# Strassen's identity for the gate and value products of the last two blocks, with GpSimd making sums

## The chip, the cores and the metric

The kernel runs on one core of one Trainium2 chip. The metric is the device time of one execution in microseconds. The core has five engines with queues of their own: TensorE (PE; its weight loads are shown as PEld), VectorE (DVE), ScalarE (ACT), GpSimd (POOL) and SyncE (SP, which issues most DMAs here). Each engine works through its own queue in order and waits for the others through semaphores.

## The reference

Linear attention with cosine weights, followed by a gated feed-forward layer:

```
phi(x) = [relu(x) * cos, relu(x) * sin]           # cos, sin of the position; 64 -> 128 features
kv  = phi(k)^T v ;  z = sum over positions of phi(k)
x   = (phi(q) kv) / (phi(q) z + 1e-6)             # 8 batches x 8 heads x 576 positions x 64
g   = x @ w_gate ;  val = x @ w_val               # x: 4608 x 512, weights 512 x 1536
out = (gelu(g) * val) @ w_out                     # w_out: 1536 x 512
```

Inputs and output are float32; the kernel multiplies in bf16 and accumulates in float32.

## The kernel before

The 4608 tokens of x are cut into nine blocks of 512 (NB = 9). For each block, `gv_unit` makes 128 of the 1536 columns of gate and value: four matmuls of 512 columns with w_gate into one PSUM bank and four with w_val into the next (line 401), then gelu on ACT (line 409), then the multiply on DVE that writes `hT` (line 410). Twelve such units (jt = 0 to 11) make a block. The units alternate between banks 0 and 1 and banks 2 and 3, so a unit may start once the unit before the last has been read out.

The output product of a block is made while the next block's units run. It already uses Strassen's identity in Winograd's form: per half p of a block, seven products of 128 x 768 by 768 x 256 in place of eight. `product` (line 510) issues six matmuls of 256 columns; ACT copies some of the results (line 530), DVE adds them (line 524). The sums of parts of `hT` that the products need, S1 to S4 for each p, are made by `h_sum` on DVE (line 494), and the sums T1 to T4 of w_out were made once, in block 1. PSUM banks 4 and 5 hold the products.

The order of the work is written out by hand: the program order of the loops is the order in each engine's queue (`manual_schedule`), and the semaphore waits follow from the tiles that are read and written. A tile pool with `bufs=2` gives the same two buffers in turn; a new tile of a name waits until the readers of the tile two before it are done. An engine whose next instruction has all its waits fulfilled may run ahead of the others; nothing else ties it to a place in the loop.

The attention of the batches is spread over the blocks before they are needed: DVE and ACT make phi(q) and phi(k) (lines 163 and 161), DVE casts v (line 180), PE makes kv (line 242) and the numerators (line 283), DVE divides (lines 294 to 296), and DMA transposes on SP's queue turn x into `xT` (line 350). This work ends in block 6 (n = 6); blocks 7 and 8 only have gate, value and output products. SP's queue also stores the outputs (line 421). POOL issues the early loads of weights and inputs, until 45 us, and computes nothing after that.

After the last unit, fourteen products of the last block remain: the tail, written as a list at the end of the program. For that block S1, S2 and S4 are made in two pieces, the larger one ahead of the last unit, the rest (the last two jt) in the tail; their place is the free input buffers of q, k and v (`place`).

The lines of the change are `place` and `h_sum` (lines 473 to 494), the main loop (from line 743) and the tail (from line 826).

Of the kernel before, what the change touches and what calls it, by code (L numbers as in the profile page):

```python
# [9 lines left out]
FP32 = mybir.dt.float32  # L10
BF16 = mybir.dt.bfloat16
AF = mybir.ActivationFunctionType
ALU = mybir.AluOpType
# [3 lines left out]
def kernel(  # L17
# [13 lines left out]
    nc = tc.nc  # L31

    B, H, S, D = q.shape
    F = 2 * D
    C = H * D
    J = moe_w_gate.shape[1]
    CT = C // 128
    JT = J // 128
    NP = H // 2
    R = S // 64  # L40
    NB = B * S // 512
    NT = 5
    EPS = 1e-6
    BLK = 512
# [6 lines left out]
    inp = ctx.enter_context(tc.tile_pool(name="inp", bufs=2))  # L51
    attn = ctx.enter_context(tc.tile_pool(name="attn", bufs=1))
# [12 lines left out]
    def bank(i):  # L65
        return ps[:, i]
# [356 lines left out]
    def flush(engs=(nc.sync, nc.sync)):  # L423
        for i, o_sb in stores:
            store(engs, i, o_sb)
        stores.clear()
# [45 lines left out]
    def place(n, p, name, cols, dtype):  # L472

        if n < NB - 1:
            return sums.tile([128, cols], dtype, name=name)
        was = "q" if name[0] == "u" else "kv"[p]
        if was not in rest:
            n_el = 8 * CH if was == "q" else 4 * JH * 128
            rest[was] = [inp.tile([128, n_el], dtype, name=was + "f"), 0]
        t, at = rest[was]  # L480
        rest[was][1] += cols
        return t[:, at:at + cols]

    def h_sum(n, p, name, j0=0, j1=JH):
        a = hs.setdefault((n, p), h_parts(n, p))
        if name not in a:
            a[name] = place(n, p, name, JH * 128, BF16).rearrange("q (j t) -> q j t", j=JH)
        x, y, op = {
            "S1": ("A21", "A22", ALU.add),
            "S2": ("S1", "A11", ALU.subtract),  # L490
            "S3": ("A11", "A21", ALU.subtract),
            "S4": ("A12", "S2", ALU.subtract),
        }[name]
        nc.vector.tensor_tensor(a[name][:, j0:j1], a[x][:, j0:j1], a[y][:, j0:j1], op=op)  # L494

    PROD = {
        1: ("A11", "B11"), 2: ("A12", "B21"), 3: ("S4", "B22"), 4: ("A22", "T4"),
# [5 lines left out]
    def product(n, p, i, u, m, v):  # L503


        a, b = PROD[i]
        key = n, p
        at = {1: u, 6: u, 7: u, 5: m, 3: m, 2: v, 4: v}[i]
        for j in range(JH):
            nc.tensor.matmul(  # L510
                at,
                lhsT=hs.setdefault(key, h_parts(n, p))[a][:, j],
                rhs=ts[b][:, j],
                start=(j == 0 and i in (1, 2, 4, 5)),
                stop=(j == JH - 1),
                skip_group_check=i in (3, 6, 7),
            )
        if key not in got:
            got[key] = [outp.tile([128, C], FP32, name="o_sb") for _ in range(2)]
        lo, hi = got[key]  # L520
        last = n == NB - 1

        def add(o, k, x, op=ALU.add):
            nc.vector.tensor_tensor(o, got[key, k], x, op=op)  # L524

        if i in (1, 6, 7) or last and i == 5:
            if last and i == 7:
                add(hi[:, RIGHT], 5, u)
            got[key, i] = place(n, p, f"u{i}", CH, FP32)
            nc.scalar.copy(got[key, i], at)  # L530
        if i == (2 if last else 1):
            add(lo[:, LEFT], 1, v)
        if i == 7 and not last:
            add(hi[:, RIGHT], 7, m)
        if i == 4:
            add(hi[:, LEFT], 7, v, ALU.subtract)
        if i == 3:
            add(lo[:, RIGHT], 6, m)
        if i in (3, 4):
            flush()  # L540
            stores.append((4 * n + 2 + p, hi) if i == 4 else (4 * n + p, lo))
            if last:
                flush((nc.sync, nc.scalar if p == 1 and i == 4 else nc.sync))


    HALF = BLK // 2
# [193 lines left out]
        (2, 1): ((8,), ()),  # L740
    }
    turn[0] = 1
    for n in range(1, NB):
        b = n + 1

        t_kv, t_nm, t_turn = {1: (7, 9, 12), 2: (6, 7, 11), 3: (2, 5, 9)}.get(n, (1, 2, 8))
        for jt in range(JT):
            if n == 1 and jt >= t_nm:
                nm_unit(2, jt - t_nm, (6, 4, 6)[jt - t_nm])
                turn_x(2, jt - t_nm)  # L750
            heads = (0, 2, 4, 2)[n] if n < 4 else 0
            if n == NB - 1 and jt in (8, 9):
                h_sum(n, jt - 8, "S3")
            if n == NB - 1 and jt == JT - 1:
                for p in range(2):
                    for name in ("S1", "S2", "S4"):
                        h_sum(n, p, name, 0, JH - 2)
            if jt >= heads:
                gv_unit(n, jt)
            else:  # L760
                for i in range(2):
                    half, unit = divmod(2 * jt + i, heads)
                    gv_unit(n, unit, half * HALF, HALF)
                    if n == 1:
                        j = JA + 2 * jt + i
                        prep("q", b, 1, (j,), eng=nc.scalar)
                        prep("q", b, 0, (j,))
                        if jt == i == 0:
                            turn_x_pe(1, 3, 5, act_copy)
            if n > 1:  # L770
                p, u = divmod(jt, 6)
                for i in ((2, 1), (5,), (6,), (7,), (4,), (3,))[u]:
                    product(n - 1, p, i, ps[:, 4, 0:CH], ps[:, 5, 0:CH], ps[:, 4, CH:C])
                for i in map(int, SUMS[n].get(jt, "")):
                    h_sum(n - 1, i // 5, f"S{(i - 1) % 4 + 1}")
            if jt % 3 == 1:
                flush()
            if b < B:
                if n == 1 and jt == 2:
                    prep("q", b, 0, (R - 1,))  # L780
                    prep("q", b, 1, (R - 1,), eng=nc.scalar)
                    turn_q(b)
                    nm_unit(1, NT - 1)
                if n == 1 and jt == 3:
                    turn_x(1, NT - 1)
                nms = [(b, jt - t_nm)] if n > 1 and 0 <= jt - t_nm < NT else []
                if n == 2 and jt < 2:
                    nms.append((n, 3 + jt))

                late = -(-(BLK - 64 * b) // 128)  # L790
                i = jt - t_nm - 1
                if n > 1 and 0 <= i < late:
                    turn_x(b, i)
                if n == 1 and jt == JT - 1:
                    loads(3, ("k", "v"))
                for bt in nms:
                    nm_unit(*bt)
                if jt == t_kv:
                    kv_unit(b)
                if n == 1 and jt in (2, 3, 4):  # L800
                    prep_third("k", b, jt - 2)
                if n == 1 and jt == 5:
                    cast_v(b, 0, 4, dve_copy)
                if (n, jt) in q3:
                    cosines, sines_ = q3[n, jt]
                    prep("q", 3, 1, sines_, eng=nc.scalar)
                    prep("q", 3, 0, cosines)
                for name, c, what in COMING.get(n, {}).get(jt, ()):
                    if name == "v":
                        cast_v(c, what, what + 2, dve_copy)  # L810
                    else:
                        prep(name, c, 0, what)
                        prep(name, c, 1, what, eng=nc.scalar)
                c = {(2, 1): 2}.get((n, jt), b if n > 1 and jt == t_turn else None)
                if c is not None:
                    if c + 1 < B:
                        turn_q(c + 1)
                    if c + 2 < B:
                        loads(c + 2)
                    for i in range(-(-(BLK - 64 * c) // 128), NT):  # L820
                        turn_x(c, i)
            if n == 1 and 4 <= jt < 8:
                wo_sum(f"T{jt - 3}")


    for what in (
        ["S1", "S2", "S4", (0, 1), (1, 1), (0, 2, 0 + 2 * (turn[0] % 2)), (0, 5), (0, 6)]
        + ["T1", "T2", "T4", (1, 2, 1 + 2 * (turn[0] % 2)), (0, 3), (0, 7), (1, 5), (0, 4, 0)]
        + [(1, 6), (1, 3), (1, 7), (1, 4, 1)]
    ):  # L830
        if isinstance(what, str):
            h_sum(NB - 1, "ST".index(what[0]), "S" + what[1], JH - 2, JH)
        else:
            p, i = what[:2]
            to = (what[2:] or (0,))[0]
            product(
                NB - 1, p, i, ps[:, 4 + 2 * p, 0:CH], ps[:, 5 + 2 * p, 0:CH], ps[:, to, 0:CH]
            )


# [28 lines left out]
```

## Time and profile before

| what | value |
|---|---|
| median of 3 runs | 318.86 us (318.25 to 319.17) |
| the profiled execution | 319.06 us, of which the profile's span is 316.9 us |
| PE busy | 306.9 us, 97% |
| DVE busy | 224.7 us, 71% |
| ACT busy | 159.4 us, 50% |
| POOL busy | 26.0 us, 8%, all in the first 50 us |
| granted TensorE clock | 0.996 |
| gate and value matmuls (line 401) | 881 recorded, means of 363 and 364 ns |
| product matmuls (line 510) of 256 columns | mean of 273 ns |
| multiply into hT (line 410) | mean 648 ns |
| product copy on ACT (line 530), sum on DVE (line 524) | means 372 and 418 ns, 256 columns |
| sum of hT parts (line 494), 768 columns | mean 552 ns |

Matmuls are pipelined, so the mean time of one record is longer than the distance to the next. The chain of waits gives the pace: it lists stretches of PE work with their length and the number of matmuls in them. PE's last matmul of a gate-and-value unit ends at 302.4 us; the tail of fourteen products takes 9.18 us after that.

### The profile page before, as it was taken

To read this page: it belongs to the slowest core of one execution; us is meant where nothing else is said; L and a number is where in the kernel's file an instruction comes from. 1 tells how busy PE (TensorE), PEld (TensorE's weight loads), DVE (VectorE), ACT (ScalarE), POOL (GpSimd) and SP (SyncE) were. 2 spreads that over 40 slices of the span, in tenths; PEclk is the share of its full clock that TensorE was granted. 3 is DMA by queue.
4 is the path that set the end of the run, shared out by engine and by line. 5 is a ranking of instruction groups with operands and counts; after the bars stand their busy time and mean duration, and the time that the engine had idled before them with its cause. 6 is when DMAs were issued, how large, how long until landed. Compare 5 with 4: busy or idle time off the path is not lost.

```text
span 316.9 us, 7015 instructions
## 1 busy us (share of the span) xinstructions
PE 306.9 (97%) x2692; PEld 191.8 (61%) x2727; DVE 224.7 (71%) x542; ACT 159.4 (50%) x356; POOL 26.0 (8%) x43
## 2 busy tenths in 40 slices
PE   8899999999999999999999999999999999999994
PEld 2574455655866676666665566556666565656583
DVE  5854695699897996798687859695944554454782
ACT  7864675956474754466328632773232323232321
POOL 6674430000000000000000000000000000000000
PEclk9999999999999999999999999999999999999998
DMA  7999999871798946995993699175342020202025
GB/s 268 245 178 245 312 320 402 259 149 38 241 202 300 304 99 179 370 163 133 319 272 88 152 369 232 34 150 109 76 86 50 17 68 0 66 2 67 2 67 132
DMA packets 68945, 53.61 MB, mean 169 GB/s; under 512 B 45360, under 2 KB 54064, under 8 KB 68912
## 3 DMA queue, kind: packets, MB, share of 16 engines
q1 hardware_dynamic: 59184, 41.23, 49.7%
q0 software_dynamic: 9648, 11.80, 16.1%
q8 instruction: 21, 0.34, 0.4%
q10 hardware_dynamic: 80, 0.13, 0.1%
q14 instruction: 12, 0.10, 0.1%
HBM read 37.75 MB, written 9.44 MB: 149 GB/s over the span
## 4 chain that ended last, share of the span: by engine, by line
PE 86%; DMA 8%; issue 1%; DVE 1%; POOL 1%; SPq 0%; ACT 0%; DVEq 0%; POOLq 0%
PE ps L401 56%; PE ps L510 23%; DMA qf<-in_q_dram 4%; PE ps L283 3%; PE ps L242 2%; DMA vf<-in_v_dram 2%; DMA wv_sb<-in_moe_w_val_dram 2%; PE ps L373 1%; PE ps L431 1%; PE ps L358 0%; DVE x_sb L296 0%; SPq L81 0%; POOL wg_sb L95 0%; DVE o_sb L524 0%; POOL gate L560 0%
## 5 line engine op out<-in xcount | busy, mean ns | idle before, releaser
L410 DVE TENSOR_TENSOR hT<-gel,ps 128x512 bf16<-128x512 f32 (+1 forms) x114 | 73.5, 648 | 55.8 <-PE ps L401 50.3
L401 PE MATMUL ps<-xT,wv_sb 128*128 128x512 bf16 (+1 forms) x450 | 109.4, 364 | 0.3
L401 PE MATMUL ps<-xT,wg_sb 128*128 128x512 bf16 (+1 forms) x431 | 107.4, 363 | 1.5 <-issue 0.3
L409 ACT ACTIVATE gel<-ps 128x512 f32<-128x512 f32 (+1 forms) x114 | 64.4, 566 | 78.6 <-PE ps L401 72.3
L401 PEld LDWEIGHTS <-wv_sb 128*128 128x128 bf16 x456 | 44.6, 98 | 47.1
L401 PEld LDWEIGHTS <-wg_sb 128*128 128x128 bf16 x456 | 41.7, 98 | 28.2 <-issue 0.3
L510 PEld LDWEIGHTS <-S 128*128 128x128 bf16 x336 | 32.9, 98 | 14.9 <-DVE S L494 0.9
L530 ACT COPY u<-ps 128x256 f32<-128x256 f32 x42 | 15.6, 372 | 43.4 <-PE ps L510 43.4
L510 PE MATMUL ps<-T,S 128*128 128x256 bf16 x252 | 34.4, 273 | 0.0
L161 ACT ACTIVATE qp<-qf,sin_t 128x256 bf16<-128x256 f32 x72 | 32.0, 501 | 3.7 <-DMA qf<-in_q_dram 3.7
L524 DVE TENSOR_TENSOR o_sb<-u,ps 128x256 f32<-128x256 f32 x56 | 23.4, 418 | 14.4 <-ACT u L530 14.4
L510 PEld LDWEIGHTS <-hT 128*128 128x128 bf16 x288 | 28.2, 98 | 8.8
L161 ACT ACTIVATE kp<-kf,sin_t 128x256 bf16<-128x256 f32 (+1 forms) x73 | 30.0, 480 | 1.0 <-DMA kf<-in_k_dram 1.0
L296 DVE TENSOR_TENSOR x_sb<-ps,rec 128x512 bf16<-128x512 f32 x38 | 26.3, 692 | 2.0 <-DMA xT<-x_sb 0.5
L163 DVE TENSOR_SCALAR qp<-qf,cos_t 128x256 bf16<-128x256 f32 x71 | 22.0, 357 | 3.3 <-DMA qf<-in_q_dram 3.3
L510 PE MATMUL ps<-wo_sb,hT 128*128 128x256 bf16 x192 | 23.6, 273 | 0.0
L163 DVE TENSOR_SCALAR kp<-kf,cos_t 128x256 bf16<-128x256 f32 x63 | 18.2, 349 | 0.0
L283 PEld LDWEIGHTS <-qT 128*128 128x128 bf16 x304 | 14.6, 98 | 2.8 <-ACT qT L588 0.3
L283 PE MATMUL ps<-kv_sb,qT 128*128 128x65 bf16 x304 | 16.0, 194 | 0.0
L494 DVE TENSOR_TENSOR S<-hT 128x768 bf16<-128x768 bf16 x28 | 15.4, 552 | 0.0
L510 PE MATMUL ps<-T,hT 128*128 128x256 bf16 x96 | 13.1, 273 | 0.2
L180 DVE CAST vx<-vf 128x1152 bf16<-128x1152 f32 (+1 forms) x15 | 11.9, 802 | 1.0 <-DMA vf<-in_v_dram 1.0
(84 smaller groups left out, 204.8 us busy)
## 6 DMA issues: line engine op xcount, KB each, us to landing
out_dram<-o_sb SPq DMA_DIRECT2D x71, 128.0 KB, 2.5
kf<-in_k_dram SPq DMA_DIRECT2D x12, 576.0 KB, 7.2
vf<-in_v_dram SPq DMA_DIRECT2D x12, 576.0 KB, 8.7
qf<-in_q_dram SPq DMA_DIRECT2D x10, 576.0 KB, 5.2
qf<-in_q_dram POOLq DMA_DIRECT2D x4, 576.0 KB, 12.4
kf<-in_k_dram POOLq DMA_DIRECT2D x4, 576.0 KB, 12.5
vf<-in_v_dram POOLq DMA_DIRECT2D x4, 576.0 KB, 12.6
wg_sb<-in_moe_w_gate_dram POOLq DMA_DIRECT2D x6, 256.0 KB, 6.8
```

The costliest lines, as they stand in the source:

```text
L161: nc.scalar.activation(o, i, AF.Relu, scale=tab[:, j:j + 1])
L163: (eng or nc.vector).tensor_scalar(o, i, 0.0, tab[:, j:j + 1], op0=ALU.max, op1=ALU.mult)
L180: copy(vx_tiles[b % 2][:, m0:m1, j0:j1, 0:D], staged["v", b][:, m0:m1, j0 * D:j1 * D].rearrange("p m (j d) -> p m j d", d=D),)
L283: nc.tensor.matmul(bank(b0 + h // 4)[:, (h % 4) * (D + 1):(h % 4 + 1) * (D + 1)], lhsT=q_cols(b, t, h), rhs=kv_sb[b][:, h // 2, h % 2, :], ...
L296: nc.vector.tensor_tensor(x, nm[:, :, :, 0:D], rec[:, :, :, None].to_broadcast([128, 2, 4, D]), op=ALU.mult,)
L401: nc.tensor.matmul(bank(b0 + g)[:, 0:w], lhsT=wt[:, ct, js], rhs=xt[:, ct, c0:c0 + w], start=(ct == 0), stop=(ct == CT - 1),)
L409: nc.scalar.activation(gel[:, 0:w], bank(b0)[:, 0:w], AF.Gelu)
L410: nc.vector.tensor_mul(hT[n][:, jt, c0:c0 + w], gel[:, 0:w], bank(b0 + 1)[:, 0:w])
L494: nc.vector.tensor_tensor(a[name][:, j0:j1], a[x][:, j0:j1], a[y][:, j0:j1], op=op)
L510: nc.tensor.matmul(at, lhsT=hs.setdefault(key, h_parts(n, p))[a][:, j], rhs=ts[b][:, j], start=(j == 0 and i in (1, 2, 4, 5)), stop=(j == ...
L524: nc.vector.tensor_tensor(o, got[key, k], x, op=op)
L530: nc.scalar.copy(got[key, i], at)
```

## The change

Blocks 7 and 8 (`FAST = NB - 2`) no longer use `gv_unit`. Gate and value together are one product of the stacked weights (w_gate over w_val) with x, and Strassen's identity is applied to its halves: the weights' rows are gate or value, the contraction is cut in two (ct 0 and 1, ct 2 and 3), and the block's tokens in two halves of 256. A unit then has seven products of two matmuls of 256 columns each, in place of eight matmuls of 512 columns.

- `w_sum` makes the sums S1 to S4 of the weights on POOL, in twelve pieces of 128 x 1024, written into the loop of block 6 (one in each jt). They lie in the freed input buffers of q, k and v.
- `x_sum` makes T1 to T4 of a block's `xT` on DVE, 128 x 512 each: for block 7 in block 6 at jt 8 to 11, for block 8 in block 7 at jt 2, 4, 6 and 8.
- `fast_unit(t, between)` runs the products of unit t, spread over two units: products 1, 5, 6, 2 and 3 of unit t, and 7 and 4 of unit t - 1. P1 is copied by ACT into the place of P2 in PSUM, and P2 accumulates on it; P6 and P7 and P4 accumulate on P1's bank, P3 on P5's. The out-projection's product of the step before (`o_step`) stands between.
- `h_sum` takes an engine; in blocks 7 and 8 the S sums of `hT` go to POOL. The small rest in the tail stays on DVE.
- The temporaries of the products lie in the buffers of `qT`, `qp` and `kp`; the tail begins inside the last half unit, with (0, 1) ahead of the last P4 and (1, 1) after it.

The core of the diff:

```diff
-    def h_sum(n, p, name, j0=0, j1=JH):
+    def h_sum(n, p, name, j0=0, j1=JH, eng=nc.vector):
...
-        nc.vector.tensor_tensor(a[name][:, j0:j1], a[x][:, j0:j1], a[y][:, j0:j1], op=op)
+        eng.tensor_tensor(a[name][:, j0:j1], a[x][:, j0:j1], a[y][:, j0:j1], op=op)
...
+    def w_sum(name, j0, j1):
+        if not wa:
+            wa["A11"], wa["A12"] = wg_sb[:, 0:CP], wg_sb[:, CP:CT]
+            wa["A21"], wa["A22"] = wv_sb[:, 0:CP], wv_sb[:, CP:CT]
+        if name not in wa:
+            was = {"S1": "qf", "S2": "qf", "S3": "kf", "S4": "vf"}[name]
+            wa[name] = inp.tile([128, CP, J], BF16, name=was)
+        x, y, op = {
+            "S1": ("A21", "A22", ALU.add),
+            "S2": ("S1", "A11", ALU.subtract),
+            "S3": ("A11", "A21", ALU.subtract),
+            "S4": ("A12", "S2", ALU.subtract),
+        }[name]
+        nc.gpsimd.tensor_tensor(
+            wa[name][:, :, j0:j1], wa[x][:, :, j0:j1], wa[y][:, :, j0:j1], op=op
+        )
...
+    GV = {
+        1: ("A11", "B11"), 2: ("A12", "B21"), 3: ("S4", "B22"), 4: ("A22", "T4"),
+        5: ("S1", "T1"), 6: ("S2", "T2"), 7: ("S3", "T3"),
+    }
...
+    def fast_unit(t, between):
+        def at(i, t):
+            if i == 2:
+                return ps[:, 0, 256 * (t % 2):256 * (t % 2) + 256]
+            return bank((3, 1)[t % 2] if i in (3, 5) else (2, 6, 7)[t % 3])[:, 0:256]
+
+        def mm(i, t):
+            n, jt = FAST + t // JT, t % JT
+            a, b = GV[i]
+            for ct in range(CP):
+                nc.tensor.matmul(
+                    at(i, t),
+                    lhsT=wa[a][:, ct, jt * 128:(jt + 1) * 128],
+                    rhs=xb[n][b][:, ct],
+                    start=(ct == 0 and i in (1, 5)),
+                    stop=(ct == CP - 1),
+                    skip_group_check=i not in (1, 5),
+                )
...
+        if new:
+            mm(1, t)
+            nc.scalar.copy(at(2, t), at(1, t))
+            mm(5, t)
+            nc.scalar.copy(tmp(M5, t), at(5, t))
+        if old:
+            mm(7, t - 1)
+            gelu(t - 1, 1, tmp(G2, t - 1))
+            nc.vector.tensor_tensor(tmp(V2, t - 1), tmp(M5, t - 1), at(7, t - 1), op=ALU.add)
+        between()
+        if old:
+            nc.vector.tensor_tensor(
+                h(t - 1, 1), gels[t - 1][:, 256:512], tmp(V2, t - 1), op=ALU.mult
+            )
+        if new:
+            mm(6, t)
+            nc.scalar.copy(tmp(U6, t), at(6, t))
+            mm(2, t)
+            gelu(t, 0, at(2, t))
+            mm(3, t)
+            nc.vector.tensor_tensor(tmp(G2, t), tmp(U6, t), at(3, t), op=ALU.add)
+        if old:
+            mm(4, t - 1)
+            nc.vector.tensor_tensor(
+                h(t - 1, 0), gels[t - 1][:, 0:256], at(4, t - 1), op=ALU.mult
+            )
...
-    for n in range(1, NB):
+    for n in range(1, FAST):
...
+            if n == FAST - 1:
+                w_sum(f"S{jt // 3 + 1}", 512 * (jt % 3), 512 * (jt % 3) + 512)
+                if jt >= 8:
+                    x_sum(FAST, jt - 8)
+
+    def o_step(n, jt):
+        p, u = divmod(jt, 6)
+        for i in ((2, 1), (5,), (6,), (7,), (4,), (3,))[u]:
+            product(n - 1, p, i, ps[:, 4, 0:CH], ps[:, 5, 0:CH], ps[:, 4, CH:C])
+        for i in map(int, SUMS[n].get(jt, "")):
+            h_sum(n - 1, i // 5, f"S{(i - 1) % 4 + 1}", eng=nc.gpsimd)
+        if jt % 3 == 1:
+            flush()
+
+    for t in range(2 * JT):
+        n, jt = FAST + t // JT, t % JT
+        if n == NB - 1 and jt in (9, 10):
+            h_sum(n, jt - 9, "S3", eng=nc.gpsimd)
+        if n == NB - 1 and jt == JT - 1:
+            for p in range(2):
+                for name in ("S1", "S2", "S4"):
+                    h_sum(n, p, name, 0, JH - 2, eng=nc.gpsimd)
+        fast_unit(t, lambda: o_step(FAST + (t - 1) // JT, (t - 1) % JT) if t else None)
+        if n == FAST and jt in (2, 4, 6, 8):
+            x_sum(NB - 1, jt // 2 - 1)
...
+    def ends():
+        o_step(NB - 1, JT - 1)
+        last_product(0, 1)
+
+    fast_unit(2 * JT, ends)
...
-        ["S1", "S2", "S4", (0, 1), (1, 1), (0, 2, 0 + 2 * (turn[0] % 2)), (0, 5), (0, 6)]
-        + ["T1", "T2", "T4", (1, 2, 1 + 2 * (turn[0] % 2)), (0, 3), (0, 7), (1, 5), (0, 4, 0)]
-        + [(1, 6), (1, 3), (1, 7), (1, 4, 1)]
+        [(1, 1), "S1", "S2", "S4", (0, 2, 0), (0, 5), (0, 6), "T1", "T2", "T4"]
+        + [(1, 2, 1), (0, 3), (0, 7), (1, 5), (0, 4, 0), (1, 6), (1, 3), (1, 7), (1, 4, 1)]
```

## The prediction

> **What bounds the kernel now.** I read the page first (engines, slices, chain, groups), then the chain of waits in order of time, the busy time by stretches, and the timelines of the stretches that the change touches. From the page:
>
> ```profile
> span 316.9 us, 7015 instructions
> PE 306.9 (97%) x2692; PEld 191.8 (61%) x2727; DVE 224.7 (71%) x542; ACT 159.4 (50%) x356; POOL 26.0 (8%) x43
> ...
> DVE  5854695699897996798687859695944554454782
> ...
> POOL 6674430000000000000000000000000000000000
> ...
> PE ps L401 56%; PE ps L510 23%; DMA qf<-in_q_dram 4%; PE ps L283 3%; PE ps L242 2%; DMA vf<-in_v_dram 2%; DMA wv_sb<-in_moe_w_val_dram 2%; PE ps L373 1%; PE ps L431 1%; PE ps L358 0%; DVE x_sb L296 0%; SPq L81 0%; POOL wg_sb L95 0%; DVE o_sb L524 0%; POOL gate L560 0%
> ```
>
> PE never rests. POOL is empty after the sixth slice (7.9 us each); DVE is full in the middle and half empty in the last ten slices. In the chain, in order of time, start and length of one gate-and-value unit and of one product:
>
> ```profile
> 278.63 1.73 PE ps L401 x8
> 280.36 0.66 PE ps L510 x6
> ```
>
> Eight matmuls of 512 columns take 1.73 us (0.216 each), six of 256 take 0.66 (0.109 each), each with its own weight load of 98 ns hidden. The last two blocks fill 242 to 302.4 us. The busy time by stretches for one piece of it:
>
> ```profile
> 270.00:280.00 10.00, 9.95 (x62) 5.99 (x62) 4.77 (x9) 2.63 (x5) 0.00 (x0) 1.00 0.23 54
> ```
>
> PE 9.95 of 10 at full clock, DVE 4.8, ACT 2.6, POOL nothing. Less PE work here shortens the kernel, if nothing makes PE wait.
>
> **What the Trainium skill says.** "GPSIMD Engine Reference", section 3.1: a two-input sum on POOL took 4497 ns for 2048 elements a partition, about twice DVE. No such sum is in this trace. "SBUF — State Buffer", section "Who interferes with whom": DVE and GpSimd share a port pair, taken as a lock for a whole instruction, by a DVE instruction in a two-port mode (casts and scalar operations from SBUF) or with two SBUF inputs, against a GpSimd one that reads SBUF. The only place where this trace has both is the start (timeline, start and us):
>
> ```profile
> 4.54 1.86 POOL L163 TENSOR_SCALAR kp<-kf,sin_t 128x128 bf16<-128x128 f32 x1 [2.17 <-DMA kf<-in_k_dram]
> 5.81 0.51 DVE L170 SCALAR_TENSOR_TENSOR kp<-kf,sin_t 128x256 bf16<-128x256 f32 x1
> 6.24 0.41 DVE L170 SCALAR_TENSOR_TENSOR kp<-kf,sin_t 128x256 bf16<-128x256 f32 x1
> ```
>
> POOL needed 1.86 us for 128 columns while DVE ran two-input operations back to back, and the first of two equal DVE operations took 0.10 us more. That agrees with a lock, though weakly: POOL read only 128 columns, so DVE paid little. A two-input sum of 1024 elements would read for all of its two microseconds.
>
> **Part 1, fewer columns.** A unit goes from 8 × 0.216 = 1.73 us to 14 × 0.109 = 1.53: 0.20 saved, times 24 units, **-4.8 us**. Products per block, the tail's 14 products (9.18 us in the chain) and the stores stay.
>
> **Part 2, the new combining work.** Per unit ACT gets five 256-column instructions for one of 512, and half a product copy as before: 5.5 × 0.37 (row L530) = 2.0 us by durations, 1.5 by start to start (two copies in a row take 0.65). DVE gets four for one, and 8 product sums a block: 4.7 × 0.42 (row L524) = 2.0 us, 1.5 by start to start (0.33). The new cycle is 1.53 + 14 × 0.66 / 12 = 2.30 us, so PE still sets it. The tightest wait: P4 of the previous unit overwrites the bank that V2 reads. With PE's unit at 0, P7 ends at 0.66, the product at 1.31, P4 starts at 1.97. V2 follows the previous unit's last multiply on DVE, at about 1.0, and ends at 1.4: 0.55 to spare. U6's copy ends near 1.95 and the next P7 wants it at 2.6. Product sums and the gelu of the other half queue behind V2, and are not nearer. Bounds 0 to 1; I take **+0.3**. The x sums (8 of 512 bf16, 0.42 each) fall where DVE waits 1.0 to 1.7 us a unit; cost nothing. The second block's need xT at about 248 us; the last transpose is issued at 233.6 and the slowest landed in 10.4. No DMA is added and no queue is passed: POOL issues none after 45 us.
>
> **Part 3, the weight sums on POOL.** Twelve of 1024 elements, estimated from the skill's figure at 2.25 us each. They are written in block 6, but POOL's queue is bound only by its waits: S1 takes the slot of q of batch 6, free when ACT's last read ends (173.0), the other nine follow q of batch 7 (203.80 + 1.71 = 205.5). So nine sums run from 205.5 to some 230, where DVE is busiest. From the timelines:
>
> ```profile
> 203.80 1.71 ACT L161 ACTIVATE qp<-qf,sin_t 128x256 bf16<-128x256 f32 x4
> ...
> 206.95 0.87 DVE L163 TENSOR_SCALAR kp<-kf,cos_t 128x256 bf16<-128x256 f32 x3
> ...
> 208.94 0.87 DVE L163 TENSOR_SCALAR kp<-kf,cos_t 128x256 bf16<-128x256 f32 x3
> 209.72 0.76 DVE L180 CAST vx<-vf 128x1152 bf16<-128x1152 f32 x1
> ...
> 214.45 0.55 DVE L494 TENSOR_TENSOR S<-hT 128x768 bf16<-128x768 bf16 x1
> ...
> 215.06 0.72 PEld L510 LDWEIGHTS <-S 128*128 128x128 bf16 x6 [0.15 <-DVE S L494]
> ```
>
> Three groups of prep (three scalar operations, a cast with the second and third) are two-port, then S1 of block 5's h has two SBUF inputs; and PE waits 0.15 us for that S1 already, so each microsecond by which it is late is PE's. By hand, with the lock granted in the order of asking and POOL asking again 0.5 us after it ends: the first group waits from 206.95 to 207.8; the second until 10.9, its cast until 14.0; the third until 16.95, its cast until 20.05; S1 until 23.0 (all + 200) and is done at 223.5 instead of 215.0, 8.5 us late. If each group waits just once, for half a sum: four waits of 1.1 less 1.2 us of idle time in DVE there, 3.3. Without a lock 0. I take **+6**. The three sums at 173 meet nine prep operations and two casts at 174.4 to 180.3; units reuse their banks after about 2.9 us, which covers one wait of 2.25 but not two: 0 to 2.5, **+1**.
>
> **Part 4, h sums moved to POOL.** Eight a block of 768 elements, estimated 1.7 us each for DVE's 0.55. S1 is wanted 3.7 us after h is complete in block 7 and 2.5 in block 8; POOL makes it, by 0.8 there; at 2.6 us it would be 0.1 late. But DVE's multiply of gel and V2 has two SBUF inputs, and everything behind it on DVE (G2, the other multiply, V2 of the next unit, for which P4 waits) moves with it. A wait of up to 1.7 meets 0.55 of cover: the first of a run of sums costs up to 1.2, later ones less, as DVE then follows POOL's rhythm. Two runs, 0 to 3.5 us, **+1.5**. In the tail, POOL's six of 512 elements (1.1 each) run beside DVE's last sums, on which products 5 and 6 wait with about 0.4 us of cover: 0 to 2.5, **+1**.
>
> **Sum:** -4.8 + 0.3 + 6 + 1 + 1.5 + 1 = +5.0. The profiled execution took 319.06 us (span 316.9 and 2.2 around it), so 324.1, and against the median of 318.86, 0.2 lower, **324**.
>
> **Rivals.** *The lock costs little* (chance 0.33): arbitration by burst, a faster sum, or POOL yielding. DVE's 0.10 us at the start speaks for it, POOL's 1.86 against. Then -4.8 + 0.3 + up to 2: 314.4 to 316.5, say 315, faster. It decides at the S1 of 214.45: all lock costs under 3.5 us together make the kernel faster. *DVE nearly holds its own* (0.08): each group waits once; 3.3 + 1 there and elsewhere against 4.5 gained, 318 to 319.8, no change. *DVE becomes the bound in the last blocks without any lock* (0.08): V2 later than its 0.55 of cover by 0.1 to 0.4 in each of 24 units, 2.4 to 10 us, 317 to 324; against it, 1.5 to 2.0 of 2.3 us. *Alternation* (0.09): each two-port operation waits out a sum of its own, eleven times 2.0 us less slack, +12 or more: 331. *The forecast* (0.42): 320 to 330.
>
> **How the numbers follow.** 0.3% of 318.86 (1.0 us) is about what a measurement here can tell from no change. Faster is the first rival and a little of the third, 0.34; same 0.07; slower 0.59. The likeliest case gives 324, its own range 320 to 330. The range must take in the first rival: 314.2 to 330 leaves out alternation and the lowest end, under 2 in 10.
>
> **What would show it.** Right: POOL busy from 173 and from 205.5 on; prep scalar operations and casts there with durations of 1 to 2.5 us in place of 0.35 and 0.76; PE waiting for the S1 of block 6; stretches 242 onward 4 us shorter, yet with DVE waits. Wrong if prep durations hold at 0.35 with POOL busy beside them: then the gain stands. POOL sums far from 2.25 us move every lock term with them; sums of 4.5 would also end after block 7 begins.

## The result, and the profile after

The changed kernel took 334.9 us (median of four runs, 334.41 to 335.17) against 318.56 us for the kernel before beside it (317.65 to 319.17): ratio 1.0514, 95% interval 1.0483 to 1.0544. The profiled span grew from 316.9 to 333.4 us. The forecast was 324.0 us with a range of 314.2 to 330, so the direction was right and the size was not.

From the page of the changed kernel: the engines, three of the lines by fortieths of the span (8.3 us each), and three groups (busy us and mean ns of one behind the bar):

```profile
span 333.4 us, 7614 instructions
PE 308.6 (93%) x2871; PEld 205.8 (62%) x2871; DVE 263.9 (79%) x598; ACT 183.0 (55%) x452; POOL 89.5 (27%) x79
...
PE   8799999999999999999997999818999989999984
...
DVE  5854677898997967986889687898684898888892
...
POOL 5675310000000000000025000994000851194660
...
L568 POOL TENSOR_TENSOR qf<-wv_sb 128x1024 bf16<-128x1024 bf16 x3 | 6.4, 2150 | 128.8 <-ACT qp L161 128.8
...
L163 DVE TENSOR_SCALAR kp<-kf,cos_t 128x256 bf16<-128x256 f32 x63 | 34.2, 600 | 0.0
...
L642 DVE TENSOR_TENSOR hT<-gel,qT 128x256 bf16<-128x256 f32 x24 | 19.2, 799 | 0.8
```

PE's busy time hardly moved (306.9 to 308.6), but PE now rests: the "1" in the 27th slice stands under the second run of POOL work. The prep's scalar operation on DVE (L163) went from a mean of 349 ns to 600. In time order, the chain of waits passes through DVE at that place, and later shows the new unit at its length:

```profile
217.45 4.32 DVE kp L163 x2
221.77 2.59 DVE vx L180
...
280.44 1.53 PE ps L604 x14
```

So the unit did become 0.20 us shorter (1.73 to 1.53), as intended. Where the time went is read from the same instruction in both traces. A ledger of how late the changed kernel is (a matmul is taken to end one step of PE's pace after its start; the last column is rounded from unrounded times):

| the same instruction in both traces | before | after | late by | added in this step |
|---|---|---|---|---|
| DVE multiply for hT, ahead of the first POOL sums | 173.47 | 173.56 | 0.1 | 0.1 |
| DVE multiply for hT, past the three sums at 173 | 206.02 | 209.24 | 3.2 | 3.1 |
| last gate-and-value matmul of block 6 ends, past the nine sums | 242.5 | 258.3 | 15.8 | 12.6 |
| last matmul of all ends, past blocks 7 and 8 and the tail | 312.1 | 328.5 | 16.4 | 0.7 |

Nearly all of the loss, 15.7 of 16.4 us, comes in the two stretches of POOL's weight sums (6.4 us from 173.1 on, 19.6 us from 208.9 on), and none of it on PE's own instructions. The timelines of POOL and of DVE in the second stretch (start, us, engine, line, operation, count; in brackets the idle time before it):

```profile
208.85 6.39 POOL L568 TENSOR_TENSOR qf<-qf,wg_sb 128x1024 bf16<-128x1024 bf16 x3 [29.33 <-ACT qp L161]
215.21 6.41 POOL L568 TENSOR_TENSOR kf<-wg_sb,wv_sb 128x1024 bf16<-128x1024 bf16 x3
221.58 6.88 POOL L568 TENSOR_TENSOR vf<-wg_sb,qf 128x1024 bf16<-128x1024 bf16 x3
```

```profile
210.17 5.22 DVE L163 TENSOR_SCALAR kp<-kf,cos_t 128x256 bf16<-128x256 f32 x3
215.31 0.68 DVE L410 TENSOR_TENSOR hT<-gel,ps 128x512 bf16<-128x512 f32 x1
215.91 0.41 DVE L524 TENSOR_TENSOR o_sb<-u,ps 128x256 f32<-128x256 f32 x1
216.24 5.52 DVE L163 TENSOR_SCALAR kp<-kf,cos_t 128x256 bf16<-128x256 f32 x3
221.69 2.67 DVE L180 CAST vx<-vf 128x1152 bf16<-128x1152 f32 x1
...
225.21 3.66 DVE L163 TENSOR_SCALAR kp<-kf,cos_t 128x256 bf16<-128x256 f32 x3
```

Three scalar operations take 5.22 and 5.52 us in place of 0.87, the cast 2.67 in place of 0.76. Above the times of before that is 4.35 + 4.65 + 1.91 + 2.79 = 13.7 us, of which idle time that DVE had there swallowed 1.1: 12.6. The multiply and the block sum between them, which read PSUM and at most one operand from SBUF, kept their 0.68 and 0.41 us. The prep's operations between 207 and 232 us (count, shortest, median and longest ns) give the rule:

```profile
L163 DVE TENSOR_SCALAR kp<-kf,cos_t x9: 341/2199/2211, 210.2 to 228.5; 128x256 bf16<-128x256 f32 x9
```

2199 ns is one POOL sum of 2150. The first operation of each group took 0.96 to 1.28 us, as it waited out the rest of a running sum; those behind it took 2.20 to 2.21, each a whole sum of its own; the last, at 228.5 past the end of POOL's sums, took its 0.34. Two neighbours among these operations and the POOL sum between them, one record each:

```profile
211.05 2.21 DVE L163 TENSOR_SCALAR kp<-kf,cos_t 128x256 bf16<-128x256 f32 x1
213.07 2.17 POOL L568 TENSOR_TENSOR qf<-qf,wg_sb 128x1024 bf16<-128x1024 bf16 x1
213.18 2.21 DVE L163 TENSOR_SCALAR kp<-kf,cos_t 128x256 bf16<-128x256 f32 x1
```

POOL's next sum starts 0.11 us before DVE's next operation does. DVE has only one operation waiting at a time, and whenever the next one comes, another sum stands ahead of it.

Such waits are the exclusive lock of the Trainium skill, "SBUF — State Buffer", section "Who interferes with whom", and the cases match the section: scalar operations and casts blocked, operations with at most one SBUF input not. It says too that the one that issues first decides who blocks; what happens when POOL has a queue of sums is what this trace adds. The same skill, "Perfetto Trace Analysis", section "GPSIMD Engine Instruction", warns that a POOL duration is unreliable and should be read start to start; here both agree (215.21 - 208.85 is 6.36 for three, 2.12 each). So POOL lost next to nothing by the scalar operations. By the longer cast it did lose; the sum behind it took half a microsecond more:

```profile
223.70 2.63 POOL L568 TENSOR_TENSOR vf<-wg_sb,qf 128x1024 bf16<-128x1024 bf16 x1
```

PE's timeline of the changed kernel shows what the late DVE did to it:

```profile
216.90 0.71 PE L510 MATMUL ps<-wo_sb,hT 128*128 128x256 bf16 x5
225.01 1.68 PE L510 MATMUL ps<-wo_sb,hT 128*128 128x256 bf16 x7 [7.40 <-DVE hT L410]
...
230.99 0.83 PE L510 MATMUL ps<-T,S 128*128 128x256 bf16 x6 [0.89 <-DVE S L494]
```

A product of block 5 stood 7.40 us for an h whose multiply was queued behind the second group and its cast. The matmuls after it ran at about half speed (the granted clock from 220 to 230 us was 0.52), but that cost nothing further, since PE then waited 0.89 us for DVE's S1 all the same.

### The profile page after: what moved, and what is told of

It is laid out like the page before. It is cut to its first block, busy times and chain, and to the rows that moved or that the text cites. A ratio compares the mean times of both kernels' runs of the same rounds, so it can differ in the third digit from the quotient of the medians.

```text
span 333.4 us, 7614 instructions
## 1 busy us (share of the span) xinstructions
PE 308.6 (93%) x2871; PEld 205.8 (62%) x2871; DVE 263.9 (79%) x598; ACT 183.0 (55%) x452; POOL 89.5 (27%) x79
## 4 chain that ended last, share of the span: by engine, by line
PE 74%; DVE 14%; DMA 4%; issue 3%; ACT 2%; POOL 1%; SPq 0%; DVEq 0%; ACTq 0%
PE ps L401 38%; PE ps L510 18%; PE ps L604 8%; DVE kp L163 5%; PE ps L431 3%; PE ps L283 3%; PE ps L242 3%; DMA vf<-in_v_dram 2%; DVE hT L642 2%; DMA wv_sb<-in_moe_w_val_dram 2%; DVE o_sb L524 1%; DVE vx L180 1%; DVE hT L410 1%; ACT qp L161 1%; DVE qT L651 1%
## 5 line engine op out<-in xcount | busy, mean ns | idle before, releaser
L401 PE MATMUL ps<-xT,wv_sb 128*128 128x512 bf16 (+1 forms) x360 | 86.4, 363 | 2.6 <-DVE hT L410 2.6
L401 PE MATMUL ps<-xT,wg_sb 128*128 128x512 bf16 (+1 forms) x360 | 86.5, 363 | 0.5 <-ACT u L530 0.5
L410 DVE TENSOR_TENSOR hT<-gel,ps 128x512 bf16<-128x512 f32 (+1 forms) x90 | 56.8, 635 | 32.0 <-PE ps L401 27.5
L409 ACT ACTIVATE gel<-ps 128x512 f32<-128x512 f32 (+1 forms) x90 | 50.2, 558 | 55.6 <-PE ps L401 50.7
L401 PEld LDWEIGHTS <-wv_sb 128*128 128x128 bf16 x360 | 35.4, 98 | 39.3 <-issue 4.3
L568 POOL TENSOR_TENSOR qf<-wv_sb 128x1024 bf16<-128x1024 bf16 x3 | 6.4, 2150 | 128.8 <-ACT qp L161 128.8
L163 DVE TENSOR_SCALAR kp<-kf,cos_t 128x256 bf16<-128x256 f32 x63 | 34.2, 600 | 0.0
L494 POOL TENSOR_TENSOR S<-hT 128x768 bf16<-128x768 bf16 x8 | 13.6, 1705 | 44.5 <-PE ps L604 43.9
L163 DVE TENSOR_SCALAR qp<-qf,cos_t 128x256 bf16<-128x256 f32 x71 | 21.6, 351 | 2.3 <-ACT kv_sb L251 2.0
L642 DVE TENSOR_TENSOR hT<-gel,qT 128x256 bf16<-128x256 f32 x24 | 19.2, 799 | 0.8
L604 PE MATMUL ps<-qp,qf 128*128 128x256 bf16 x96 | 18.3, 272 | 0.3 <-ACT ps L633 0.3
L604 PE MATMUL ps<-xT,wg_sb 128*128 128x256 bf16 x96 | 18.3, 272 | 0.0
```

The source lines that it names most:

```text
L163: (eng or nc.vector).tensor_scalar(o, i, 0.0, tab[:, j:j + 1], op0=ALU.max, op1=ALU.mult)
L401: nc.tensor.matmul(bank(b0 + g)[:, 0:w], lhsT=wt[:, ct, js], rhs=xt[:, ct, c0:c0 + w], start=(ct == 0), stop=(ct == CT - 1),)
L409: nc.scalar.activation(gel[:, 0:w], bank(b0)[:, 0:w], AF.Gelu)
L410: nc.vector.tensor_mul(hT[n][:, jt, c0:c0 + w], gel[:, 0:w], bank(b0 + 1)[:, 0:w])
L494: eng.tensor_tensor(a[name][:, j0:j1], a[x][:, j0:j1], a[y][:, j0:j1], op=op)
L604: nc.tensor.matmul(at(i, t), lhsT=wa[a][:, ct, jt * 128:(jt + 1) * 128], rhs=xb[n][b][:, ct], start=(ct == 0 and i in (1, 5)), stop=(ct == ...
```

## The experiments

The theory after the result: a run of POOL sums lets in one two-port DVE operation per sum (alternation), and this, not the new units, is the loss. Rivals: the new units make DVE or ACT the bound in the last blocks; the h sums on POOL are the main cost; the loss is the transfers or the place of the sums and not the lock.

**The weight sums alone** (kernel before; the function `w_sum` as in the change, with its tiles in the same slots):

```diff
+            if n == FAST - 1:
+                w_sum(f"S{jt // 3 + 1}", 512 * (jt % 3), 512 * (jt % 3) + 512)
```

> The kernel before with the twelve weight sums on POOL added and nothing else of the change; their results are not used. Theory (port lock, one DVE operation let in per POOL sum): the whole loss of blocks 4 to 6, 3.1 + 12.6 us, comes back: 334 us, prep operations on DVE of 2.2 us at 174 to 180 and 209 to 228. Rival (the new units of blocks 7 and 8 and their waits are to blame, DVE's lag before is only moved): no change from before, 318.6. Rival (POOL and DVE share the port without a lock): 320 to 324.

Measured 334.17 us, ratio 1.0478 (1.0455 to 1.0502). DVE's timeline of this run is the changed kernel's over again:

```profile
209.79 5.22 DVE L163 TENSOR_SCALAR kp<-kf,cos_t 128x256 bf16<-128x256 f32 x3
...
215.86 5.53 DVE L163 TENSOR_SCALAR kp<-kf,cos_t 128x256 bf16<-128x256 f32 x3
```

Twelve POOL instructions, with no other part of the change, make 15.4 us of the 16.3. The rivals that put it into the new units fall.

**The weight sums on DVE** (changed kernel):

```diff
-        nc.gpsimd.tensor_tensor(
+        nc.vector.tensor_tensor(
             wa[name][:, :, j0:j1], wa[x][:, :, j0:j1], wa[y][:, :, j0:j1], op=op
```

> The changed kernel with the twelve weight sums on DVE in block 6 in place of POOL. Theory: the 15.7 us of blocks 4 to 6 go, twelve sums of about 0.7 us find room in block 6: 319 to 320.5, with the 5 us of waits in the last blocks still there. Rival (the new units are to blame): 330 or more.

Measured 320.27 us, ratio 1.0043 (1.0027 to 1.0059). A sum takes DVE 0.68 us, as the first three do (count, shortest, median and longest ns, first and last start):

```profile
L568 DVE TENSOR_TENSOR qf<-wv_sb x3: 683/686/689, 215.0 to 221.5; 128x1024 bf16<-128x1024 bf16 x3
```

Only the last, which met an h sum on POOL, took 2.02. The last gate-and-value matmuls of block 6 start at 241.95, 0.3 us after those of the kernel before (241.64). The loss of 15.8 us there is gone with the same sums, of the same operands, at the same place in the program. It is POOL's part in them that costs. The time changed with the engine, though: DVE comes to these sums from 215.0 us on, when its prep is done. The run with the sums held back moves the time and keeps the engine.

**Half-size sums** (changed kernel, 24 sums of 512 elements):

```diff
-                w_sum(f"S{jt // 3 + 1}", 512 * (jt % 3), 512 * (jt % 3) + 512)
+                for c in (512 * (jt % 3), 512 * (jt % 3) + 256):
+                    w_sum(f"S{jt // 3 + 1}", c, c + 256)
```

> The changed kernel with each weight sum in two halves of 512 elements: 24 sums of 1.1 us. Theory (each two-port operation of DVE waits for one whole POOL sum): eleven waits of 1.1 in place of 2.2 us, so half the lag or less: 324 to 328. Rival (DVE loses what POOL is busy in all, some 26 us, however it is cut): 334 to 335.

Measured 327.78 us (326.14 to 330.39), ratio 1.0286 (1.0222 to 1.035). The line of the prep beside the later sums, the same nine operations as above:

```profile
L163 DVE TENSOR_SCALAR kp<-kf,cos_t x9: 343/1237/1246, 209.5 to 219.6; 128x256 bf16<-128x256 f32 x9
```

The median fell from 2199 to 1237 ns as a POOL sum fell from 2.16 to 1.20 us, and block 6 ended 8.7 us late (250.35 against 241.64) in place of 15.8. POOL had the same elements to sum. What an operation pays follows the length of one POOL instruction, not POOL's total work: this is alternation, one operation to one sum.

**The sums held back** (changed kernel; POOL's queue waits, ahead of its first weight sum, for the last cast of v, at 212.7 us):

```diff
             if n == FAST - 1:
+                if jt == 0:
+                    nc.gpsimd.tensor_copy(gate, vx_tiles[1][:, 3, R - 1, 0:1])
                 w_sum(f"S{jt // 3 + 1}", 512 * (jt % 3), 512 * (jt % 3) + 512)
```

> The changed kernel with POOL held by one small copy until DVE's last cast of v (about 213 us), so that the weight sums run in block 6, where DVE has no two-port operation left, only its h sums with two SBUF inputs. Theory: at most one wait of up to 2.2 us for each of some eight h sums, half of them covered, and S4 perhaps 1 to 2 us late for block 7: 321 to 327. Rival (two-input sums wait no less and everything is only moved): 332 or more.

Measured 323.25 us, ratio 1.0132 (1.0112 to 1.0153). All twelve sums now run from 212.99 to 240.6, past the prep, and block 6 ends 3.0 us late (244.67). The rest of the lock is on DVE's h sums with two SBUF inputs (and on one x sum, 1.63 us). From the timelines of DVE and, in the last line, POOL:

```profile
216.05 1.87 DVE L494 TENSOR_TENSOR S<-S,hT 128x768 bf16<-128x768 bf16 x1
...
217.85 2.47 DVE L494 TENSOR_TENSOR S<-hT 128x768 bf16<-128x768 bf16 x1
...
224.60 0.55 DVE L494 TENSOR_TENSOR S<-hT 128x768 bf16<-128x768 bf16 x1
224.66 2.48 POOL L568 TENSOR_TENSOR qf<-qf,wg_sb 128x1024 bf16<-128x1024 bf16 x1
```

An h sum takes 0.55 us free and up to 2.47 behind a POOL sum. The one at 224.60 started 0.06 us ahead of POOL's next sum and took its 0.55, so the one that asks first goes first. POOL pays here too: eight of its twelve sums took 2.43 to 2.48 us in place of 2.12, as many as there are h sums beside them. One copy of a single element per partition took 11.6 us off the kernel. It is where the sums met DVE's two-port work that cost most.

**Nothing on POOL** (the kernel with the weight sums on DVE, and the h sums of blocks 7 and 8 on DVE as well):

```diff
-            h_sum(n - 1, i // 5, f"S{(i - 1) % 4 + 1}", eng=nc.gpsimd)
+            h_sum(n - 1, i // 5, f"S{(i - 1) % 4 + 1}")
...
-            h_sum(n, jt - 9, "S3", eng=nc.gpsimd)
+            h_sum(n, jt - 9, "S3")
...
-                    h_sum(n, p, name, 0, JH - 2, eng=nc.gpsimd)
+                    h_sum(n, p, name, 0, JH - 2)
```

> The changed kernel with all sums on DVE: the weight sums as in the run before, and the h sums of blocks 7 and 8 too, so that POOL computes nothing. Theory (the waits in the last blocks are the lock's as well, on the multiply of gel and V2): PE's waits there go, most of the 4.8 us saved is seen, less some for a full DVE in block 6: 314 to 316. Rival (the chain of copies, sums and gelus of a unit is itself too long for PE): 318 to 320.5, hardly better than with the h sums on POOL.

Measured 319.36 us (317.39 to 320.78), ratio 1.0015 (0.9998 to 1.0032): a miss by 3.4 us, inside the range of the rival. The trace shows another cause than the rival's. DVE's timeline of this run ahead of the last unit, then PE's:

```profile
298.22 0.42 DVE L494 TENSOR_TENSOR kf<-hT 128x512 bf16<-128x512 bf16 x1
...
300.38 0.42 DVE L494 TENSOR_TENSOR vf<-hT,vf 128x512 bf16<-128x512 bf16 x1
300.73 0.41 DVE L639 TENSOR_TENSOR qT<-qT,ps 128x256 f32<-128x256 f32 x1
```

```profile
301.19 0.38 PE L604 MATMUL ps<-qp,wv_sb 128*128 128x256 bf16 x2 [2.30 <-DVE qT L639]
```

The six sums that POOL had made ahead of the tail now stand in one row in DVE's queue before the next V2 (L639), and PE waits 2.30 us for it. Then the clock fell, in this execution of 320.28 us. PE's stretches after the wait (us in the stretch, busy us and count of PE, PEld, DVE, ACT and POOL; the third number from the right is the granted clock):

```profile
301.00:303.00 2.00, 1.81 (x15) 1.54 (x15) 2.00 (x7) 0.42 (x1) 0.00 (x0) 0.88 0.19 44
303.00:305.00 2.00, 2.00 (x11) 1.35 (x10) 1.42 (x6) 0.37 (x1) 0.00 (x0) 0.50 0.70 162
305.00:307.00 2.00, 2.00 (x16) 1.61 (x14) 0.87 (x3) 0.39 (x2) 0.00 (x0) 0.77 0.25 56
307.00:309.00 2.00, 2.00 (x21) 1.79 (x19) 1.01 (x4) 0.73 (x2) 0.00 (x0) 1.00 0.01 4
```

If the clock is either 1.00 or 0.50, the numbers 0.88, 0.50 and 0.77 come to about 0.5, 2.0 and 0.9 us at half speed: some 3.4 us, from 302.5 on, 1.3 us after the wait ended. The 96 matmuls from 301.19 on took 12.15 us where 96 at 0.109 take 10.5. The wait and the clock together are 2.30 + 1.65 = 3.95 us, about the miss.

The fall seems not to come in every execution of this kernel. Nine of the 22 had a mean granted clock of 0.996 or more and took 317.39 to 319.11 us (median 318.1); thirteen had 0.985 to 0.995 and took 318.9 to 320.78 (median 320.0). That suggests that the wait alone leaves 318.1, 2.1 us above the forecast, and that the clock adds some 1.8 us in part of the executions. Whether this is the order of one queue or a limit of DVE is tried in the run with the late sums spread.

**The sums held back, and the h sums on DVE** (the two edits together):

```diff
+                if jt == 0:
+                    nc.gpsimd.tensor_copy(gate, vx_tiles[1][:, 3, R - 1, 0:1])
...
-                    h_sum(n, p, name, 0, JH - 2, eng=nc.gpsimd)
+                    h_sum(n, p, name, 0, JH - 2)
```

with the other two `eng=nc.gpsimd` left out as in the run before.

> The weight sums on POOL, held until DVE's last cast of v, and the h sums of blocks 7 and 8 on DVE. Theory: block 6 loses 3.0 us as in the run with late sums (323.25), and the last blocks gain what the run without POOL gains: 316 to 318. Rival: as in that run, 322 to 323.

Measured 322.79 us, ratio 1.0128 (1.0096 to 1.0159), a miss by nearly 5 us, inside the range of the rival. Block 6 loses its 3 us as it did with POOL held back alone, and the wait of 2.30 us and the fall of the clock to 0.50 are there again (PE starts again at 304.03, and the clock from 306 to 308 us was 0.50). The expectation left out both, as that of the kernel with nothing on POOL did.

**The h sums on POOL alone** (kernel before, the h sums of blocks 7 and 8 moved):

```diff
-    def h_sum(n, p, name, j0=0, j1=JH):
+    def h_sum(n, p, name, j0=0, j1=JH, eng=nc.vector):
...
-        nc.vector.tensor_tensor(a[name][:, j0:j1], a[x][:, j0:j1], a[y][:, j0:j1], op=op)
+        eng.tensor_tensor(a[name][:, j0:j1], a[x][:, j0:j1], a[y][:, j0:j1], op=op)
...
-                h_sum(n, jt - 8, "S3")
+                h_sum(n, jt - 8, "S3", eng=nc.gpsimd)
```

and the same argument at the two other calls.

> The kernel before with the h sums of blocks 7 and 8 on POOL and nothing else of the change. Theory: DVE's multiply there takes one operand from PSUM and one from SBUF, so no lock is contended, and a sum of 1.7 us is ready in time: 318.5 to 319.5. Rival (any POOL work beside DVE costs): 322 to 325. Rival (the longer sums are late for the products): 320 to 322, with PE waiting on POOL.

Measured 318.4 us, ratio 0.9991 (0.9979 to 1.0002). POOL takes 1.64 us for a sum of 768, and PE isn't delayed: with the old units, DVE in these blocks multiplies out of PSUM with one operand from SBUF, and such a multiply took the same 0.69 us beside a POOL sum as without one. Only in the tail do the two meet; DVE's sums of 256 columns there, from the timeline:

```profile
303.07 1.18 DVE L494 TENSOR_TENSOR kf<-hT 128x256 bf16<-128x256 bf16 x1
304.28 1.20 DVE L494 TENSOR_TENSOR kf<-kf,hT 128x256 bf16<-128x256 bf16 x1
305.51 0.29 DVE L494 TENSOR_TENSOR kf<-hT,kf 128x256 bf16<-128x256 bf16 x1
```

1.2 us in place of 0.29, each behind one POOL sum of 1.15. So h sums on POOL are harmless in themselves; they need an operation with two SBUF inputs on DVE to do harm. Blocks 7 and 8 of the changed kernel have two kinds: gel times V2 (L642) and the x sums (L584).

**Nothing on POOL, with the late sums spread** (the kernel with nothing on POOL; of the six sums in one row one stays, two go behind the last block's first product, and three are made whole in the tail):

```diff
-            for p in range(2):
-                for name in ("S1", "S2", "S4"):
-                    h_sum(n, p, name, 0, JH - 2)
+            h_sum(n, 0, "S1", 0, JH - 2)
...
+        for name in ("S2", "S4"):
+            h_sum(NB - 1, 0, name, 0, JH - 2)
...
-            h_sum(NB - 1, "ST".index(what[0]), "S" + what[1], JH - 2, JH)
+            h_sum(NB - 1, "ST".index(what[0]), "S" + what[1], 0 if what[0] == "T" else JH - 2, JH)
```

> The run without POOL, with the six sums of the last block (0.42 us each, 2.5 us in a row ahead of the last unit's V2) spread: one stays there, two go into the last half unit, the three of p = 1 are made whole in the tail. Theory: in the run without POOL the new units kept pace with PE, and the gain was lost only there, in a PE wait of 2.3 us and some 1.6 us of slower clock after it; without it 315 to 316.5. Rival (the units' own chain of copies and sums eats the gain): 318.5 to 320, no better.

Measured 316.12 us (315.4 to 316.73), ratio 0.9921 (0.9902 to 0.994). This is faster than both kernels. From its page and from the line of the multiply of gel and V2:

```profile
PE 303.1 (97%) x2842; PEld 205.4 (65%) x2871; DVE 250.1 (80%) x631; ACT 183.8 (59%) x452; POOL 28.0 (9%) x43
```

```profile
L642 DVE TENSOR_TENSOR hT<-gel,qT x24: 417/421/429, 247.7 to 301.0; 128x256 bf16<-128x256 f32 x24
```

All 24 of the multiplies take the same 0.42 us. The new units with all their sums fit on DVE, and the rival of the run with nothing on POOL, that a unit's own chain is too long for PE, falls.

**The h sums on POOL, with the late sums spread** (the kernel with the weight sums on DVE, and the edit of the run before; the spread sums are DVE's):

```diff
-                    h_sum(n, p, name, 0, JH - 2, eng=nc.gpsimd)
+            h_sum(n, 0, "S1", 0, JH - 2)
...
+        for name in ("S2", "S4"):
+            h_sum(NB - 1, 0, name, 0, JH - 2)
```

> As the run before, but the h sums of blocks 7 and 8 on POOL, the weight sums and the six late sums on DVE. Theory: POOL's sums of 1.7 us hold up DVE's multiply of gel and V2, which has two SBUF inputs, and PE waits behind it: 2 to 4 us worse than without POOL, 317.5 to 319.5. Rival (the h sums on POOL cost nothing here either, as in the kernel before): 315 to 316.5, the same.

Measured 318.07 us, ratio 0.998 (0.9969 to 0.999). The same line, and two of PE's waits for V2 (L639) with the operation on DVE that came before each, from the timelines:

```profile
L642 DVE TENSOR_TENSOR hT<-gel,qT x24: 415/426/1692, 250.0 to 304.7; 128x256 bf16<-128x256 f32 x24
```

```profile
246.75 1.86 DVE L584 TENSOR_TENSOR qp<-xT,qp 128x512 bf16<-128x512 bf16 x1
249.32 0.38 PE L604 MATMUL ps<-qp,wv_sb 128*128 128x256 bf16 x2 [0.76 <-DVE qT L639]
...
293.02 1.54 DVE L642 TENSOR_TENSOR hT<-gel,qT 128x256 bf16<-128x256 f32 x1
295.62 0.38 PE L604 MATMUL ps<-qp,wv_sb 128*128 128x256 bf16 x2 [0.53 <-DVE qT L639]
```

The theory named half of it. At 293 us it is the multiply, 1.54 us in place of 0.42, that makes the next V2 late for PE's P4. The longest wait, at 249 us, comes from an x sum of 1.86 us in place of 0.42, ahead of which the last weight sum on DVE had already taken 2.03 behind POOL's first h sum. The wait next in length, at 254.39, follows an x sum of 1.20. The h sums on POOL cost about 2.0 us (318.07 - 316.12) in blocks 7 and 8 and the tail, and what they delay are DVE's operations with two SBUF inputs, not the multiply alone.

## Why the prediction was wrong

Its sum of +5.0 us stands against +16.4 at the last matmul. By its parts:

| part of the prediction | its term, bounds | measured |
|---|---|---|
| 1, fewer columns | -4.8 | -4.7: blocks 7 and 8 and the tail are 69.6 us before, and 64.9 of pure matmul time after |
| 2, combining work | +0.3, 0 to 1 | +1.4: PE's gaps in the units with nothing on POOL |
| 3, nine sums at 205 | +6, 0 to 8.5 | +12.6 |
| 3, three sums at 173 | +1, 0 to 2.5 | +3.1 |
| 4, h sums on POOL | +1.5, 0 to 3.5 | +2.3: gaps in the units 3.7 us, less the 1.4; the x sums have a part in it |
| 4, the tail | +1, 0 to 2.5 | +1.7: gaps in the tail |

The lengths of gaps are worked out from PE's timeline: the start of a group less the starts before it at 0.109 us each. The pure matmul time is 24 units of 14 matmuls and 43 products of six at that pace.

**The step that failed is the hand queue of part 3.** The mechanism, the place, the durations of the sums (2.25 us estimated from the Trainium skill, "GPSIMD Engine Reference", section 3.1, and 2.15 measured) and the late S1 of block 5's h were right. (PE stood still earlier than forecast, 7.40 us for the multiply ahead of that S1 in the same queue, and then 0.89 us for S1 itself.) What failed is the line "with the lock granted in the order of asking and POOL asking again 0.5 us after it ends". With those 0.5 us a group of three scalar operations slips through behind one wait, and eleven two-port operations wait only some six times. In the trace POOL has no such pause: its sums start every 2.12 us at a length of 2.15, the next one starts 0.11 us ahead of DVE's next operation, and so DVE gets in one operation per sum. The order of asking was right (the h sum that asked first in the run with the sums held back went first); the pause was not there. Each group then pays twice or more. That is the rival called alternation, with its "eleven times 2.0 us less slack, +12 or more"; 12.6 came, at a chance of 0.09. The half-size sums confirm it: with sums half as long, the delay of an operation halves. The choice of 0.5 us rested on no line of the trace. The bound should have been worked out with 0 as well: by the same hand queue, one operation per sum, S1 comes some 12 us late, and with the other terms at their upper ends the sum is -4.8 + 1 + 12 + 2.5 + 3.5 + 2.5 = +16.7, which draws the range past 334.

The three sums at 173 failed by the same step. They cost 3.1 us, above the 2.5 of "one wait but not two": a single group of prep there took 5.18 us in place of 0.87, 4.3 more, of which the idle time of DVE took 1.2:

```profile
174.50 5.18 DVE L163 TENSOR_SCALAR kp<-kf,cos_t 128x256 bf16<-128x256 f32 x3
```

**Part 1** is right, and the fastest run shows it as a gain. **Part 2** was undersized: 1.4 us where 1 was the upper end. In the run that gives this number DVE makes the h sums too, so it is an upper value for the combining work alone. It consists of 0.44 us at the first unit, for ACT's copy of P1, and of starts of P4 held up by V2 as named, by 0.42, 0.37, 0.09 and 0.09 us; the other units follow each other without a gap. The two longer ones speak against "The x sums [...] cost nothing": each follows an x sum that stands right ahead of V2. DVE's timeline of the fastest kernel ahead of the first of them, an x sum (L584) and V2 (L639), and PE's P4:

```profile
250.62 0.42 DVE L654 TENSOR_TENSOR hT<-gel,ps 128x256 bf16<-128x256 f32 x1
250.95 0.42 DVE L584 TENSOR_TENSOR qp<-xT 128x512 bf16<-128x512 bf16 x1
251.28 0.42 DVE L639 TENSOR_TENSOR qT<-qT,ps 128x256 f32<-128x256 f32 x1
...
251.76 0.38 PE L604 MATMUL ps<-qp,wv_sb 128*128 128x256 bf16 x2 [0.26 <-DVE qT L639]
```

DVE has no pause there: with the h sums of the block before in the same queue, the x sum takes time from V2 and not from a wait. The rival that DVE becomes the bound without a lock thus has a grain of truth, worth about one microsecond of the +16.4. **Part 4** was right about the multiply and left out the x sums, which have two SBUF inputs as well: two of them took 1.75 and 1.20 us in the changed kernel, behind POOL's h sums. Its terms were 0.8 and 0.7 us short.

The rivals that the lock costs little or that DVE nearly holds its own are refuted by the changed kernel's own trace and by the two runs that have the twelve sums as the one difference (+15.4 us alone; -14.6 us when DVE makes them).

What stays open: why a POOL sum loses next to nothing to a scalar operation of 0.35 us, and 0.3 to 0.5 us to an h sum of 0.55 or a cast of 0.76, was seen and not explained. In the fastest kernel two gaps of 0.30 us remain where the last block ends. Both follow the late h sums that DVE still makes there. P4 of the last unit but one starts at 298.35, when V2 has ended at 298.30 behind one of them. A weight load (PEld) waits for the last multiply (L654), which stands behind the other two:

```profile
301.81 0.10 PEld L510 LDWEIGHTS <-hT 128*128 128x128 bf16 x1 [0.41 <-DVE hT L654]
```

## What to carry to other kernels

Work given to an idle engine isn't free if it shares a port with a busy one: when GpSimd has a row of SBUF sums ready, count up to one whole GpSimd instruction for each two-port or two-SBUF-input operation of DVE that meets them, and don't let a queue model give DVE a pause that no trace shows. A queue with nothing ahead of it starts as early as its buffers allow, so ask where it will run and not where it is written; a single-element copy that waits for the right event can hold it back. Before moving work off an engine, try it there in good order: here DVE takes all of the sums, if they don't stand in a row ahead of what PE waits for (six cost 2.30 us, one still 0.30).

## What the runs showed of the hardware that was not expected

- POOL sums without a pause let in DVE's two-port operations one by one. The measured time of such an operation is that of one POOL sum (2199 ns beside 2150), though alone it takes 348 ns. POOL keeps its pace of 2.12 us a sum beside these scalar operations; behind a cast a sum took 2.63, and beside DVE's h sums 2.43.
- Moving a bf16 sum of two SBUF inputs from POOL to DVE made it 3.2 times as fast (2.15 to 0.68 us for 1024 elements). The skill's section 3.1 of "GPSIMD Engine Reference" gives about two for its case, 2048 elements in float32.
- A wait of PE of only 2.30 us was followed by a granted clock of 0.50 from 1.3 us after its end, in the profiled executions of both kernels that had it, for about 3.4 us, and 1.65 us were lost. The times of the 22 executions of the first of them suggest that it doesn't happen every time. The Trainium skill, "TensorE: Matmul & The Clock Gate", Part 1, puts the idle window at some 3.4 us. The wait of 7.40 us is longer than that, though the clock fell about 2.8 us into it (0.52 from 220 to 230 us is 9.6 us at half speed, so from 220.4 on; the wait began at 217.6); the wait of 2.30 is shorter, and the measurement decides.
